# Pack attention with a gated MLP on one core: scores in the banks of h, merged with a chunk of M, and a new written order

## The chip, the cores and the metric

The kernel runs on one core of a Trainium2 chip. The metric is the device time of one launch in microseconds (us). A run of the profiler adds a trace, with the start and duration of every instruction, measured from the first instruction on; that distance from the first to the last instruction is the span. The engines of a core work side by side: TensorE (PE, with the loads of its weights as PEld), VectorE (DVE), ScalarE (ACT), GpSimd (POOL), and SyncE (SP), which here only issues DMAs. Each engine takes its instructions strictly in the order in which the program lists them, and waits on semaphores where it needs something of another.

## The reference

Eight batches, eight heads, 576 positions, head size 64. Packing queries p (32 per head) attend to k and v; the result then serves as keys and values for q. The heads side by side are x, which goes through a gated MLP with 2048 hidden units.

```python
def sm_attn(qq, kk, vv):
    s = scale * np.matmul(qq, kk.transpose(0, 1, 3, 2))
    s = s - np.max(s, axis=-1, keepdims=True)
    a = np.exp(s)
    a = a / (np.sum(a, axis=-1, keepdims=True) + 1e-09)
    return np.matmul(a, vv)
p_packed = sm_attn(p, k, v)
out = sm_attn(q, p_packed, p_packed)
...
h = x @ w_in
g = h * (1.0 / (1.0 + np.exp(-1.702 * h)))
return (g @ w_out).astype(np.float32)
```

## The kernel before

**What it multiplies.** x is never formed. For each batch the packed result P (32 rows per head) is multiplied into w_in first: M = P w_in, four chunks of 512 columns (`m_chunk`, L575). Then h = A M, with A the softmax weights of q (`hp_mm`, L795), and the output is G w_out, with G the gated h (`product`, L868, and `plain`, L874). For accuracy every operand of the large matmuls is split into an upper and a lower rounded part (`..._upper` makes the rounded copy, `..._lower` subtracts it from the value), and each product is three matmuls: hi x hi, hi x lo, lo x hi.

**Rounds.** A batch b has two rounds, n = 2b with 256 positions (even) and n = 2b + 1 with 320 (odd). In a round h is made in eight pairs p of 128 hidden units each (j = 0, 1): two `hp_mm` fill the two banks of the tile `hh`; `hp_tanh` (ACT, L804) reads both, `hp_gate` (DVE, L691) reads both again and leaves G in SBUF; `sums_1`, `sums_2`, `sums_3` (L826, L830, L834) add and subtract blocks of G, since the output is made with seven products in place of eight (a Strassen scheme with the sums of w_out prepared once); `g_upper` (L171 on ACT, L173 on DVE) and `g_lower` (L841) round G and the sums, in two pieces per pair; then come the seven `product` steps, which accumulate in four PSUM banks `acc`. At the end of a round `take_1` to `take_6` (L887 to L911) read `acc`, and `keep` (L917) stores. The odd 64 positions of the odd rounds are laid aside in DRAM (`hp_over`, L814) and go through `product` later in two rounds of their own ("over", read by `over_in`, L818). G and its rounded parts have two buffers each, taken in turn by the pairs; `hh` has one.

**Attention in between.** Of batch b + 1, the packing scores (`scores1`, two halves, L365) are made while the rounds of batch b run: `scores1_copy`, `scores1_max`, `bias1` and `exp1` work on the SBUF tile `x1`, `turn1_blocks` (L480) transposes it in 32-blocks into another tile, and eight DMAs `turn1_out` (L487) with six DMAs `turn1_in` (L498) turn it through DRAM ("aside"). `pack` (L511) multiplies with v, `pack_turn_mm` (L562) transposes P. Then the scores of q (`scores2_mm`, two halves, L617), `scores2_turn` (DVE, L625), `max2`, `sub2`, `exp2`, `sum2`, `norm2`, `turn2`, `a_upper` and `a_lower` make A for the two rounds, and the four `m_chunk` (L583) with `m_upper` (L171, L173) and `m_lower` (L598) make M. From batch 2 on, a chunk of w_in comes by one DMA (`win_in`, L297) into a ring of one buffer.

**Banks.** PSUM has eight banks of 512 columns: 0 to 3 are `acc`, 4 and 5 are h (`hh` once the pairs begin), 6 and 7 are `bb`. From batch 2 on, `scores1`, `scores2_mm`, `m_chunk`, `pack` and `pack_turn_mm` all take turns in 6 and 7.

**PE's tiles.** `hp_mm`, `product` and the like use PE's array as one tile of 128 x 128. `scores1`, `scores2_mm` and `m_chunk` use it as eight tiles of 64 x 32 (four head pairs by even and odd head), `pack` as four of 128 x 32.

**The first batch.** Here nothing runs beside the chain from the loads to the first h matmul: `scores1`, softmax, `turn1_first`, `pack_first`, `scores2_mm`, softmax, `turn2`, `a_upper`, with the first weights decoded by `begin_w` (ACT, L263) and `join_w` (DVE, L276). `warm` (L177) gives PE matmuls on the identity whose results nobody reads. For the first two rounds h is made and multiplied in single pieces (`h_mm`, `out_mm`), while all weights are decoded.

**The order.** The tuple `order` (from L926) lists every step with its engine where there is a choice. The program runs through it once, and each engine's queue is the list filtered for that engine. The order is written out in full, and no scheduler changes it.

```python
for step, *args in order:
    step(*args)
```

Of the kernel before, what the change touches and what calls it, by code (L numbers as in the profile page):

```python
# [24 lines left out]
def kernel(  # L25
# [900 lines left out]
    order = (  # L926
        (load, 'k', 0, 0), (warm, 7, 7, 4), (load, 'k', 0, 1), (load, 'v', 0, 0), (load_w, 0, 0),
        (load, 'v', 0, 1), (load, 'q', 0, 0), (load, 'q', 0, 1), (load_w, 2, 0), (load_w, 1, 0),
        (scores1, 0, 0, (6, 0)), (warm, 1, 1, 5), (load_w, 3, 0), (max1_first, 0, 0),
        (load_w, 2, 1), (max1_first, 1, 0), (load_w, 3, 1), (bias1_first, 0), (bias1_first, 1),  # L930
        (exp1_first, 0, 0), (load_w, 4), (scores1, 0, 1, (7, 1)), (exp1_first, 1, 0),
        (max1_first, 0, 1), (load, 'k', 1, 0), (turn1_first, 0, 6), (bias1, 0, 0), (load_w, 1, 1),
        (max1_first, 1, 1), (exp1_first, 0, 1), (load_w, 0, 1), (bias1, 0, 1), (warm, 3, 3, 4),
        (turn1_first_copy, 0, dve), (factor_first, 0), (factor_first, 1), (load, 'k', 1, 1),
        (exp1_first, 1, 1), (load_w, 7), (turn1_first, 1, 7), (sum1, 0, 1), (load_w, 5),
        (sum1, 0, 0), (load_w, 9), (turn1_last_mm, 0, 6), (turn1_first_copy, 1), (load_w, 6),
        (pack_first, 0), (load_w, 8), (turn1_last_copy, 0), (pack_first, 1), (load_w, 11),
        (pack_first_half, 0), (pack_first, 2), (pack_first_half, 1), (load_w, 10),
        (pack_first_end, 0), (pack_turn_mm, 0, 7), (warm, 6, 2, 5), (pack_turn_copy, 0),
        (begin_w, 0, 0), (scores2_mm, 0, 0, (6, 7)), (warm, 4, 2, 4), (join_w, 0, 0),  # L940
        (scores2_turn, 0, 0, 0), (scores2_mm, 0, 1, (2, 3)), (scores2_turn, 0, 0, 1),
        (warm, 5, 2, 5), (begin_w, 2, 0), (max2, 0, 0, 0), (warm, 8, 3, 4), (max2, 0, 0, 1),
        (begin_w, 1, 0), (scores2_turn, 0, 1, 0), (sub2, 0, 0, 1, pool), (warm, 0, 3, 5),
        (scores2_turn, 0, 1, 1), (sub2, 0, 0, 0, pool), (warm, 2, 3, 4), (max2, 0, 1),
        (exp2, 0, 0, 0), (join_w, 2, 0), (begin_w, 3, 0), (join_w, 1, 0), (exp2, 0, 0, 1),
        (sum2, 0, 0, 0), (begin_w, 3, 1), (join_w, 3, 0), (sum2, 0, 0, 1), (norm2, 0, 0, 0, pool),
        (m_chunk, 0, 0, (0, 1), 0), (m_upper, 0, 0, 1, 0), (sub2, 0, 1, None, pool),
        (turn2, 0, 0, 0), (m_upper, 0, 0, 0, 0), (m_lower, 0, 0, 1, 0), (a_upper, 0, 0, 0),
        (a_lower_mm, 0, 0, 0, 6), (norm2, 0, 0, 1), (exp2, 0, 1), (scores1, 1, 0, (5, 4)),
        (join_w, 3, 1), (turn2, 0, 0, 1), (begin_w, 4), (sum2, 0, 1), (a_upper, 0, 0, 1),  # L950
        (a_lower_copy, 0, 0, 0), (a_lower_mm, 0, 0, 1, 7), (join_w, 4), (scores1_copy, 1, 0, 1),
# [961 lines left out]
```

## Time and profile before

| What | Value |
|---|---|
| Median of three runs | 697.26 us (697.04 to 697.88) |
| Profiled execution, own time | 696.75 us |
| Its span | 694.9 us |
| Mean granted clock of PE | 0.995 |
| PE matmuls of the products, L863 | 349.3 us in 2553 |
| PE matmuls of the pairs, L698 into hh | 203.7 us in 1344 |
| PE matmuls of the chunks of M, L583 into b | 34.4 us in 512 |
| DMA, mean | 148 GB/s |

The page gives each engine's busy time and share of the span, then the 40 slices, the DMA queues, the chain that ended last, and the costliest groups. A group's row reads: line, engine, operation, output<-input with shapes, count | busy time, mean ns of one | idle time just before them and what ended it. A row of the timeline reads: start, duration, engine, line, operation and shapes, count, and in brackets the idle time before it with what ended it. The rows of one group of pipelined matmuls overlap the next by their tails, so the distance from start to start is what a group costs. A row of the waits reads: who waited, for what, the sum in us, how many times, the longest.

### The profile page before, as it was taken

How to read it: one execution, taken by the hardware profiler on the slowest of the kernel's cores; microseconds unless marked ns; L12 is line 12 of the kernel's file. 1: busy time of each engine (PE TensorE's matmuls, PEld its weight loads, DVE VectorE, ACT ScalarE, POOL GpSimd, SP SyncE). 2: the span in 40 equal slices, each digit the busy share in tenths (PEclk: the TensorE clock that was granted, in tenths of full speed). 3: DMA queues.
4: the chain of work that ended last, by engine and by line, in shares of the span. 5: the costliest groups of instructions: out<-in, count | busy, mean ns of one | idle time of the engine just before them, and what ended most of it. 6: DMA issues, size and time to landing. Idle time of an engine off the chain costs nothing. (4 is left out here: it accounts for less than half of the span.)

```text
span 694.9 us, 15468 instructions
## 1 busy us (share of the span) xinstructions
PE 671.4 (97%) x6037; PEld 594.4 (86%) x6037; DVE 594.0 (85%) x1204; ACT 309.5 (45%) x603; POOL 186.6 (27%) x202
## 2 busy tenths in 40 slices
PE   8999999999999999999989999999999999999996
PEld 6678777887879888998789998989889988899996
DVE  5998988968998889978898878998799879988895
ACT  4887645524453444434334434453435434343231
POOL 2543422510761455212331112231112112211010
PEclk9999999999999999999999999999999999999999
DMA  9997961343532545333823334642554353301042
GB/s 344 385 353 223 332 240 61 102 114 116 198 141 60 154 147 210 102 89 137 274 80 92 103 97 133 220 151 45 164 168 162 102 155 103 130 1 43 16 126 60
DMA packets 79016, 103.09 MB, mean 148 GB/s; under 512 B 53920, under 2 KB 58976, under 8 KB 74336
## 3 DMA queue, kind: packets, MB, share of 16 engines
q1 hardware_dynamic: 78944, 102.12, 44.3%
q8 instruction: 47, 0.77, 0.5%
q14 instruction: 25, 0.20, 0.1%
HBM read 80.14 MB, written 21.95 MB: 147 GB/s over the span
## 5 line engine op out<-in xcount | busy, mean ns | idle before, releaser
L863 PE MATMUL acc<-at_float32r 128*128 128x256 f32 (+1 forms) x2553 | 349.3, 292 | 4.7 <-POOL at_float32r L841 1.9
L863 PEld LDWEIGHTS acc<-at_float32r 128*128 128x128 f32 x2553 | 327.5, 192 | 15.2 <-ACT at_float32r L171 2.7
L171 ACT CAST at_float32r<-at_float 128x512 fp32r<-128x512 f32 (+3 forms) x225 | 126.2, 569 | 202.5 <-PE acc L863 101.6
L698 PEld LDWEIGHTS hh<-at_float32r 128*128 128x128 f32 x1344 | 183.8, 189 | 35.0 <-DVE at_float L834 8.2
L698 PE MATMUL hh<-at_float32r 128*128 128x256 f32 (+1 forms) x1344 | 203.7, 300 | 1.6 <-DVE at_float L691 1.5
L841 DVE TENSOR_TENSOR at_float32r<-at_float,at_float32r 128x512 fp32r<-128x512 f32 (+3 forms) x192 | 130.4, 699 | 10.6 <-ACT at_float32r L171 6.6
L804 ACT ACTIVATE at_float<-hh 128x512 f32<-128x512 f32 (+1 forms) x112 | 72.9, 651 | 99.1 <-PE hh L698 93.0
L691 DVE SCALAR_TENSOR_TENSOR at_float<-at_float,hh 128x512 f32<-128x512 f32 (+1 forms) x112 | 83.8, 748 | 27.4 <-ACT at_float L804 27.1
L841 POOL TENSOR_TENSOR at_float32r<-at_float,at_float32r 128x512 fp32r<-128x512 f32 (+3 forms) x49 | 59.0, 1207 | 130.6 <-ACT at_float32r L171 46.9
L826 POOL TENSOR_TENSOR at_float<-at_float 128x256 f32<-128x256 f32 x30 | 22.2, 740 | 157.3 <-DVE at_float L691 154.8
L173 DVE CAST at_float32r<-at_float 128x512 fp32r<-128x512 f32 (+5 forms) x100 | 41.1, 411 | 19.9 <-PE acc L863 15.6
L748 PE MATMUL acc<-at_float32r 128*128 128x512 f32 x192 | 48.1, 393 | 0.0
L598 DVE TENSOR_TENSOR at_float32r<-b,at_float32r 128x512 fp32r<-128x512 f32 (+1 forms) x64 | 41.2, 671 | 1.7 <-ACT at_float32r L171 1.6
L826 DVE TENSOR_TENSOR at_float<-at_float 128x256 f32<-128x256 f32 x83 | 39.0, 470 | 2.4
L748 PEld LDWEIGHTS acc<-at_float32r 128*128 128x128 f32 x192 | 34.8, 188 | 7.0 <-issue 0.8
L830 DVE TENSOR_TENSOR at_float<-at_float 128x128 f32<-128x128 f32 x100 | 34.2, 342 | 4.7 <-POOL at_float L826 1.9
L171 ACT CAST at_float32r<-b 128x512 fp32r<-128x512 f32 (+1 forms) x55 | 29.8, 581 | 17.5 <-PE b L583 17.5
L583 PE MATMUL b<-at_float,at_float 64*32 64x512 f32 (+1 forms) x512 | 34.4, 594 | 0.0
L698 PEld LDWEIGHTS h<-at_float32r 128*128 128x128 f32 x192 | 27.2, 189 | 7.7 <-DVE at_float L625 2.4
L698 PE MATMUL h<-at_float32r 128*128 128x256 f32 (+1 forms) x192 | 30.3, 301 | 1.3 <-DVE at_float L625 0.7
L834 DVE TENSOR_TENSOR at_float<-at_float 128x128 f32<-128x128 f32 x92 | 28.5, 310 | 2.1
L647 POOL TENSOR_TENSOR at_float<-at_float,at_float 128x512 f32<-128x512 f32 (+2 forms) x10 | 10.4, 1045 | 63.3 <-DVE at_float L641 63.3
(117 smaller groups left out, 516.4 us busy)
## 6 DMA issues: line engine op xcount, KB each, us to landing
at_float<-w_kept SPq DMA_DIRECT2D x24, 1024.0 KB, 4.8
at_float<-v SPq DMA_DIRECT2D x8, 1024.0 KB, 4.9
o<-at_float SPq DMA_DIRECT2D x32, 256.0 KB, 2.0
at_float<-w_out SPq DMA_DIRECT2D x16, 511.8 KB, 6.1
at_float<-w_in SPq DMA_DIRECT2D x12, 511.8 KB, 8.3
at_float<-k_last SPq DMA_DIRECT2D x8, 640.0 KB, 6.0
...
```

Of the source, the lines that this page charges most:

```text
L171: nc.scalar.copy(dst, src)
L173: engine.tensor_copy(dst, src)
L583: nc.tensor.matmul(banks[eo][32 * j : 32 * j + 32, columns(part)], pt(b)[rows(eo), j, :], w[rows(eo), j, columns(part)], start=True, stop= ...
L598: nc.vector.tensor_tensor(lo, t[:, at], hi.bitcast(F32), op=ALU.subtract)
L691: nc.vector.scalar_tensor_tensor(dst, th, 1.0, h, op0=ALU.add, op1=ALU.mult)
L698: nc.tensor.matmul(t[:, : NH[half]], m_part(fc, eo, mp)[:, fo : fo + P], a_part(b, half, ap, eo), start=(n == 0), stop=(n == len(terms) - 1),)
L748: nc.tensor.matmul(acc[i], g0(f, gp)[:, i * P : (i + 1) * P], wo(f, wp), start=(start and n == 0), stop=(stop and n == 2),)
L804: nc.scalar.activation(g, h, AF.Tanh, scale=1.702)
L826: engine.tensor_tensor(dst, src, by, op=ALU.subtract)
L830: engine.tensor_tensor(g_raw(n, p, 6), g_raw(n, p, 5), g_raw(n, p, 1), op=ALU.add)
L841: engine.tensor_tensor(lo, src, g_range(n, p, 0, which)[0].bitcast(F32), op=ALU.subtract)
L863: nc.tensor.matmul(acc[i][:, at : at + m], lhs, rhs, start=(start and k == 0), stop=(stop and k == len(pairs) - 1),)
```

## The change

**Banks.** Once `hh` exists, banks 4 and 5 mean its two halves. From batch 2's `scores2_mm` and batch 3's `scores1` on, the scores go there and no longer to 6 and 7. `pack`, `pack_turn_mm` and `m_chunk` stay in 6 and 7.

**Merged steps.** `both` runs two steps directly one after the other. 22 scores (`scores2_mm` of batches 2 to 7, `scores1` of batches 3 to 7, two halves each) are each joined with an `m_chunk` that follows at once: `scores2_mm` of a half with chunks 0 and 1 of the same batch, `scores1` of the next batch with chunks 2 and 3.

**Tiles.** From batch 2 on, the odd heads' first scores `x1` lie in X[3] in place of X[1], and their transposed copy in X[1] in place of X[3].

**Order and engines.** Every other step is the same in kind and number, but the order is another throughout. Products of a pair no longer come in one block of seven; products of two or three pairs mix, and may stand between the two `hp_mm` of a pair. Of the steps with a choice of engine these change: `g_lower` DVE 192 to 159 and POOL 49 to 82; `g_upper` ACT 168 to 144 and DVE 73 to 97; `sums_1` POOL 30 to 41; `sums_2` POOL 13 to 52; `sums_3` POOL 21 to 52; `a_lower` POOL 2 to 8; `sub2` POOL 10 to 13; `m_upper` DVE 10 to 16; `h_over` DVE 1 to 10; some others by a few. At the start, eighteen `warm` matmuls in place of seven stand ahead of the first `scores1`.

The diff, cut: the helpers, the start of the order, the stretch around `pack` and the first scores of batch 5, and the end.

```diff
     def bank(i):
-        return banks_all[i]
+        return pair[0][:, i - 4, :] if pair and i in (4, 5) else banks_all[i]
+
+    def both(*steps):
+        for f, *a in steps:
+            f(*a)
...
     def x1(b, eo):
-        return x_tile(eo)
+        return x_tile((0, 1 if b < 2 else 3)[eo])
+
+    def turned1(b, eo):
+        return x_tile((2, 3 if b < 2 else 1)[eo])
...
     def turn1_blocks(b, eo):
-        nc.vector.transpose(x_tile(2 + eo), x1(b, eo))
+        nc.vector.transpose(turned1(b, eo), x1(b, eo))
...
-        src = x_tile(2 + eo)[NPK * j : NPK * (j + 1), :]
+        src = turned1(b, eo)[NPK * j : NPK * (j + 1), :]
...
     order = (
-        (load, 'k', 0, 0), (warm, 7, 7, 4), (load, 'k', 0, 1), (load, 'v', 0, 0), (load_w, 0, 0),
-        (load, 'v', 0, 1), (load, 'q', 0, 0), (load, 'q', 0, 1), (load_w, 2, 0), (load_w, 1, 0),
-        (scores1, 0, 0, (6, 0)), (warm, 1, 1, 5), (load_w, 3, 0), (max1_first, 0, 0),
...
-        (exp1_first, 0, 0), (load_w, 4), (scores1, 0, 1, (7, 1)), (exp1_first, 1, 0),
...
-        (pack_first_end, 0), (pack_turn_mm, 0, 7), (warm, 6, 2, 5), (pack_turn_copy, 0),
-        (begin_w, 0, 0), (scores2_mm, 0, 0, (6, 7)), (warm, 4, 2, 4), (join_w, 0, 0),
...
-        (warm, 5, 2, 5), (begin_w, 2, 0), (max2, 0, 0, 0), (warm, 8, 3, 4), (max2, 0, 0, 1),
-        (begin_w, 1, 0), (scores2_turn, 0, 1, 0), (sub2, 0, 0, 1, pool), (warm, 0, 3, 5),
-        (scores2_turn, 0, 1, 1), (sub2, 0, 0, 0, pool), (warm, 2, 3, 4), (max2, 0, 1),
...
+        (warm, 1, 1, 5), (load, 'k', 0, 0), (warm, 7, 7, 4), (load, 'k', 0, 1), (load_w, 1, 0),
+        (load_w, 0, 0), (load, 'v', 0, 0), (warm, 6, 2, 5), (load, 'v', 0, 1), (warm, 5, 2, 5),
+        (load, 'q', 0, 0), (warm, 3, 3, 4), (load_w, 2, 0), (warm, 0, 3, 5), (load, 'q', 0, 1),
+        (scores1, 0, 0, (6, 0)), (max1_first, 0, 0), (max1_first, 1, 0), (scores1, 0, 1, (7, 1)),
+        (load_w, 3, 0), (bias1_first, 1), (bias1_first, 0), (exp1_first, 0, 0), (warm, 4, 2, 4),
+        (load_w, 3, 1), (max1_first, 1, 1), (exp1_first, 1, 0), (warm, 8, 3, 4), (bias1, 0, 1),
+        (load_w, 4), (max1_first, 0, 1), (exp1_first, 1, 1), (turn1_first, 0, 6), (bias1, 0, 0),
+        (exp1_first, 0, 1), (begin_w, 1, 0), (turn1_first, 1, 7), (turn1_first_copy, 0, dve),
+        (factor_first, 1), (begin_w, 0, 0), (sum1, 0, 1), (factor_first, 0), (turn1_last_mm, 0, 6),
+        (turn1_first_copy, 1), (load, 'k', 1, 0), (pack_first, 0), (sum1, 0, 0),
...
-        (hp_mm, 9, 2, 1), (take_6, 8), (keep, 8, 1), (turn1_in, 5, 0), (product, 9, 0, 1),
-        (turn1_in, 5, 1), (g_lower, 9, 1, 1, dve), (hp_tanh, 9, 2), (product, 9, 0, 6),
-        (turn1_in, 5, 2), (product, 9, 0, 5), (hp_gate, 9, 2), (turn1_in, 5, 3),
-        (product, 9, 0, 7), (turn1_in, 5, 4), (product, 9, 0, 2), (sums_1, 9, 2, dve),
-        (turn1_in, 5, 5), (product, 9, 0, 3), (product, 9, 0, 4), (sums_2, 9, 2, dve),
-        (hp_over, 9, 2), (sums_3, 9, 2, dve), (hp_mm, 9, 3, 0), (keep, 8, 0),
-        (g_upper, 9, 2, 0, act), (g_upper, 9, 2, 1, dve), (g_lower, 9, 2, 1, dve),
-        (hp_mm, 9, 3, 1), (g_lower, 9, 2, 0, dve), (pack, 5, (6, 7)), (hp_tanh, 9, 3),
...
-        (g_lower, 9, 3, 1, dve), (scores2_mm, 5, 0, (6, 7)), (g_lower, 9, 3, 0, dve),
...
-        (sums_2, 9, 4, dve), (m_chunk, 5, 0, (6, 7), None), (g_upper, 9, 4, 0, act), (sum2, 5, 0),
...
+        (product, 8, 6, 5), (turn1_in, 5, 2), (hp_tanh, 9, 1), (product, 8, 7, 1),
+        (turn1_in, 5, 0), (product, 8, 7, 4), (turn1_in, 5, 4), (hp_gate, 9, 1),
+        (product, 8, 7, 5), (product, 8, 7, 7), (g_lower, 9, 0, 0, dve), (hp_over, 9, 1),
+        (product, 8, 7, 2), (product, 8, 7, 6), (sums_1, 9, 1, pool), (hp_mm, 9, 2, 1),
...
+        (g_lower, 9, 1, 0, pool), (hp_mm, 9, 2, 0), (take_3, 8), (take_6, 8), (sums_2, 9, 1, pool),
+        (hp_tanh, 9, 2), (pack, 5, (6, 7)), (take_4, 8), (sums_3, 9, 1, pool), (keep, 8, 0),
...
+        (product, 9, 3, 2), (g_lower, 9, 2, 1, dve), (product, 9, 1, 6), (product, 9, 1, 3),
+        (sums_1, 9, 4, pool), (both, (scores2_mm, 5, 0, (4, 5)), (m_chunk, 5, 0, (6, 7), None)),
+        (sums_2, 9, 4, pool), (sums_3, 9, 4, pool), (sums_3, 9, 3, pool), (scores2_turn, 5, 0, 0),
+        (m_upper, 5, 0, 1, None, act), (win_in, 5, 1), (product, 9, 2, 6), (scores2_turn, 5, 0, 1),
+        (product, 9, 2, 7), (m_upper, 5, 0, 0, None, act), (g_upper, 9, 4, 0, dve),
+        (product, 9, 1, 5), (hp_mm, 9, 5, 0), (g_lower, 9, 4, 0, dve), (g_upper, 9, 3, 1, act),
...
+        (product, ('over', 1), 7, 6), (product, ('over', 1), 7, 1), (product, ('over', 1), 7, 7),
+        (take_1, ('over', 1)), (product, ('over', 1), 7, 5), (take_2, ('over', 1)),
+        (product, ('over', 1), 7, 3), (take_3, ('over', 1)), (product, ('over', 1), 6, 2),
+        (product, ('over', 1), 7, 2), (take_4, ('over', 1)), (product, ('over', 1), 6, 4),
+        (take_5, ('over', 1)), (product, ('over', 1), 7, 4), (take_6, ('over', 1)),
```

More of the change, by code (lines that the diff above doesn't have):

```diff
@@ L933 @@
[L933 to L938, printed above, removed]
@@ L945 @@
[L945 to L950, printed above, removed]
@@ new lines @@
+        (hp_over, 5, 3), (g_upper, 5, 3, 1, dve), (sums_1, 5, 4, pool), (g_lower, 5, 3, 1, pool),
+        (scores2_turn, 3, 0, 1), (m_upper, 3, 0, 1, None, act), (win_in, 3, 1), (product, 5, 3, 2),
+        (scores2_turn, 3, 0, 0), (product, 5, 2, 1), (m_upper, 3, 0, 0, None, act),
+        (m_lower, 3, 0, 1), (hp_mm, 5, 5, 1), (g_upper, 5, 4, 0, dve), (sums_2, 5, 4, dve),
+        (product, 5, 2, 7), (max2, 3, 0), (hp_mm, 5, 5, 0), (g_lower, 5, 4, 0, dve),
+        (product, 5, 2, 5), (sums_3, 5, 4, dve), (sub2, 3, 0, None, pool), (hp_tanh, 5, 5),
@@ new lines @@
+        (product, 7, 4, 4), (product, 7, 3, 3), (sums_1, 7, 6, dve),
+        (both, (scores2_mm, 4, 1, (4, 5)), (m_chunk, 4, 1, (6, 7), None)), (sums_3, 7, 5, dve),
+        (turn2, 4, 0), (sums_2, 7, 6, pool), (g_lower, 7, 5, 0, dve), (a_upper, 4, 0, None, dve),
+        (m_upper, 4, 1, 1, None, act), (load, 'k', 5, 0), (scores2_turn, 4, 1, 1),
+        (product, 7, 4, 2), (product, 7, 4, 5), (hp_over, 7, 6), (scores2_turn, 4, 1, 0),
+        (g_upper, 7, 5, 1, act), (product, 7, 4, 7), (max2, 4, 1), (win_in, 4, 2),
@@ new lines @@
+        (hp_gate, 11, 4), (product, 11, 2, 5), (product, 11, 2, 2), (g_lower, 11, 3, 0, dve),
+        (both, (scores2_mm, 6, 0, (4, 5)), (m_chunk, 6, 0, (6, 7), None)), (sums_1, 11, 4, dve),
+        (g_upper, 11, 3, 1, dve), (sums_2, 11, 4, pool), (g_lower, 11, 3, 1, pool),
+        (scores2_turn, 6, 0, 1), (win_in, 6, 1), (product, 11, 2, 7), (scores2_turn, 6, 0, 0),
+        (product, 11, 2, 6), (hp_over, 11, 4), (m_upper, 6, 0, 1, None, dve), (product, 11, 2, 4),
+        (hp_mm, 11, 5, 1), (g_upper, 11, 4, 0, act), (max2, 6, 0), (sums_3, 11, 4, dve),
@@ new lines @@
+        (both, (scores2_mm, 7, 1, (4, 5)), (m_chunk, 7, 1, (6, 7), None)),
+        (g_upper, 13, 6, 0, act), (g_lower, 13, 5, 1, dve), (hp_over, 13, 5),
+        (sums_2, 13, 6, pool), (g_lower, 13, 6, 0, pool), (scores2_turn, 7, 1, 1),
+        (m_upper, 7, 1, 0, None, act), (win_in, 7, 2), (product, 13, 4, 6), (product, 13, 5, 2),
+        (scores2_turn, 7, 1, 0), (m_upper, 7, 1, 1, None, act), (hp_mm, 13, 7, 1), (max2, 7, 1),
+        (product, 13, 5, 4), (turn2, 7, 0), (sub2, 7, 1, None, pool), (product, 13, 4, 7),
@@ L1863 @@
+        (take_5, ('over', 1)), (product, ('over', 1), 7, 4), (take_6, ('over', 1)),
+        (keep_over, ('over', 1), 1, 1), (keep_over, ('over', 1), 0, 1),
+        (keep_over, ('over', 1), 0, 0), (keep_over, ('over', 1), 1, 0),
     )
```

1786 lines of the change are left out of this document (882 added, 904 removed).

## The prediction

> **What bounds the kernel now.** I read the page's first block, then PE's waits, then its timeline.
>
> ```profile
> span 694.9 us, 15468 instructions
> PE 671.4 (97%) x6037; PEld 594.4 (86%) x6037; DVE 594.0 (85%) x1204; ACT 309.5 (45%) x603; POOL 186.6 (27%) x202
> ```
> ```profile
> PE b L511 <- DMA at_float<-aside: 5.6, 5, 1.4
> PE acc L863 <- POOL at_float32r L841: 1.9, 3, 0.8
> PE hh L698 <- DVE at_float L691: 1.5, 3, 0.7
> PE acc L863 <- DVE at_float L911: 1.1, 3, 0.4
> ```
>
> TensorE sets the time: 671.4 of 694.9 us. Its largest wait is five times for `turn1_in`'s DMAs before `pack` (5.6 us); the other rows are small. So a change pays only if it shortens PE's own work or removes one of these waits, and costs only where PE is made to wait. What PE's work costs, switches included, shows in the timeline of a steady stretch (start, duration, then the group):
>
> ```profile
> 322.78 2.68 PE L863 MATMUL acc<-at_float32r 128*128 128x256 f32 x21
> 325.30 1.93 PE L698 MATMUL hh<-at_float32r 128*128 128x320 f32 x12
> 327.06 2.68 PE L863 MATMUL acc<-at_float32r 128*128 128x256 f32 x21
> 329.67 1.09 PE L583 MATMUL b<-at_float,at_float 64*32 64x512 f32 x16
> 330.69 2.02 PE L698 MATMUL hh<-at_float32r 128*128 128x320 f32 x12
> 332.55 2.68 PE L863 MATMUL acc<-at_float32r 128*128 128x256 f32 x21
> ```
> ```profile
> 157.87 0.66 PE L617 MATMUL b<-at_float,at_float 64*32 64x256 f32 x16
> 158.47 1.15 PE L698 MATMUL hh<-at_float32r 128*128 128x320 f32 x6
> ```
>
> Seven products (21 matmuls) take 2.52 us from start to start, so one takes 0.36; two `hp_mm` (12) take 1.76. A lone chunk of M (L583) makes the group before it 0.09 longer (2.61 for 2.52), takes 1.02 itself and makes the group after it 0.10 longer (1.86): 1.21. Lone scores of 256 columns (L617) take 0.60, with the same entry and exit 0.79.
>
> **The merged blocks.** All computing steps stay (3512 when `both` is taken apart); only order, engines and places differ. 22 scores now stand directly ahead of a chunk. The kernel before has that pair already, in batch 1, on the same banks:
>
> ```profile
> 73.80 0.66 PE L617 MATMUL h<-at_float,at_float 64*32 64x256 f32 x16
> 74.26 1.06 PE L583 MATMUL b<-at_float,at_float 64*32 64x512 f32 x16
> 75.25 2.03 PE L698 MATMUL h<-at_float32r 128*128 128x320 f32 x12
> 77.12 2.23 PE L748 MATMUL acc<-at_float32r 128*128 128x512 f32 x9
> ```
>
> Scores of 256 columns take 0.46 there, the chunk 0.99, and one entry and exit 0.09 + 0.11: 1.65. Apart they take 0.79 + 1.21 = 2.00. The merge saves 0.35, and 22 x 0.35 = **-7.7 us**. Bounds: 0 (the block waits in front of its banks) to -7.7 (there is no more switching to save). What the merge asks for is that a batch's `scores1` can run while the batch before still uses its second half: its odd part now lies in X[3], no longer in X[1], where `x2` of that half is live until `turn2`. Moving the tile costs no instruction, and `turned1`, now in X[1], is written three pairs of `hp_mm` after `turn2` or later: nothing.
>
> **The aside wait.**
>
> ```profile
> 310.46 1.32 PE L511 MATMUL b<-at_float,at_float 128*32 128x64 f32 x80 [1.20 <-DMA at_float<-aside]
> ```
> ```profile
> at_float<-w_kept SPq DMA_DIRECT2D x24, 1024.0 KB, 4.8
> ```
>
> Between the last `turn1_in` and `pack` stand two `hp_mm` (1.76 us) before, and in batch 5 two products more. After, four to six products stand there: 1.4 to 2.2 us more cover, 0.7 more in batch 5. On SP's queue at most one small `hp_over` lies behind the last `turn1_in`, and as many steps of PE as before lie between the last `turn1_out` and the first `turn1_in`. The longest wait is 1.4 (the row of the waits). The other loads moved on this queue, `win_in` for the next chunk, stand at least 5.5 us of PE's work ahead of it, against 4.8 to land: nothing. Four of five go, the fifth shrinks by 0.7: **-5.1 us** (0 to -5.6).
>
> **The start.**
>
> ```profile
> 1.37 3.36 PE L177 MATMUL h<-at_float 128*128 128x128 f32 x14 [1.37 <-POOL at_float masks.py:199]
> 6.39 0.45 PE L365 MATMUL b<-at_float 64*32 64x320 f32 x1 [0.18 <-DMA at_float<-k_last]
> 14.01 0.49 ACT L263 CAST at_float<-at_float 128x256 f16<-128x256 bf16 x1 [0.78 <-DMA at_float<-w_in]
> 14.85 2.72 PE L177 MATMUL h<-at_float 128*128 128x128 f32 x22
> 22.54 0.38 PE L698 MATMUL h<-at_float32r 128*128 128x256 f32 x1 [0.16 <-ACT at_float L171]
> ```
>
> Until 22.54 the chain of the first batch sets the end, and PE's `warm` matmuls fill. Before, 14 of their matmul records stand ahead of the first scores; after, 36. The 22 more take 2.7 us (row 14.85), so the second scores, held until 6.39 by `k_last`, come at about 7.6: 1.2 later. On ACT two `begin_w` of 0.49 move ahead of the copies that `pack` needs: 1.0. `sub2` of half 0 now goes first on POOL, and joins are done earlier, which gives some back; later `begin_w` cost some. I take **+2.5**; bounds 0 (the chain absorbs it) and +4 (two more 0.49 casts, and 22 records at the first row's 3.36/14 = 0.24 each, 5.3 in place of 2.7). [...]
>
> **The banks of h.** Scores now lie in hh (banks 4, 5), which tanh and gate read. From the first product after a pair's `hp_mm`:
>
> ```profile
> 304.82 2.68 PE L863 MATMUL acc<-at_float32r 128*128 128x256 f32 x21
> 305.07 0.70 ACT L804 ACTIVATE at_float<-hh 128x640 f32<-128x640 f32 x1 [0.16 <-PE hh L698]
> 305.85 0.81 DVE L691 SCALAR_TENSOR_TENSOR at_float<-at_float,hh 128x640 f32<-128x640 f32 x1
> 274.49 2.68 PE L863 MATMUL acc<-at_float32r 128*128 128x256 f32 x21
> 275.50 0.68 DVE L691 SCALAR_TENSOR_TENSOR at_float<-at_float,hh 128x512 f32<-128x512 f32 x1
> ```
>
> hh is free after 306.66 - 304.82 = 1.84 us, with the hand-over of 0.08 (tanh's end to gate) 1.92 in an odd round; 1.7 in an even one. Before, at least seven products (2.52) cover it. After, I count 12 odd pairs with five products or fewer (1.8) to the next `hp_mm`, 9 to the scores (0.12 short), and 3 even ones with four (1.44; 0.26 short): 21 x 0.12 + 3 x 0.26 = 3.3. Behind the scores, `scores2_turn` on DVE must read both banks:
>
> ```profile
> L625 DVE STREAM_TRANSPOSE at_float<-b 128x320 f32<-128x320 f32 x12 | 5.5, 495 | 0.4
> ```
>
> Scores of 320 columns in a merged block are an estimated 0.46 x 320/256 = 0.58. With two transposes of 0.50 and hand-overs of 0.2 that is 1.8, against the scores, the chunk's 0.99 and one product or more: 1.9 at least. It holds. Less the 1.5 us (L691) of now, **+1.8** (-1.5 to +8, if each of the 22 waits 0.3 for DVE's queue).
>
> **Engines and leads.**
>
> ```profile
> L841 DVE TENSOR_TENSOR at_float32r<-at_float,at_float32r 128x512 fp32r<-128x512 f32 (+3 forms) x192 | 130.4, 699 | 10.6 <-ACT at_float32r L171 6.6
> L841 POOL TENSOR_TENSOR at_float32r<-at_float,at_float32r 128x512 fp32r<-128x512 f32 (+3 forms) x49 | 59.0, 1207 | 130.6 <-ACT at_float32r L171 46.9
> L830 DVE TENSOR_TENSOR at_float<-at_float 128x128 f32<-128x128 f32 x100 | 34.2, 342 | 4.7 <-POOL at_float L826 1.9
> L834 POOL TENSOR_TENSOR at_float<-at_float 128x128 f32<-128x128 f32 x21 | 10.4, 496 | 17.4 <-DVE at_float L830 16.6
> ```
>
> 33 `g_lower` and 70 of `sums_2` and `sums_3` go from DVE to POOL: DVE loses 33 x 0.70 + 70 x 0.34 = 47 us, POOL gains 33 x 1.21 + 70 x 0.50 = 75. Neither becomes the bound. But slack goes: from where `g_lower` stands in the order to its first product, PE's steps between come to 4.6 us (median) before, and after to 1.1 to 1.4 where DVE does it, 2.2 where POOL does. PE must wait wherever the operation is late. Nearest row: the wait for POOL L841, 1.9 us in 3. I take **+3** (0 to +23, 226 pieces of G late by 0.1).
>
> **Other waits and the tail.** The takes and the over round: of 1.1 and 1.9, **-2** (0 to -3).
>
> ```profile
> 670.25 18.32 PE L863 MATMUL acc<-at_float32r 128*128 128x256 f32 x150 [0.41 <-DVE at_float L911]
> 686.81 0.37 ACT L887 COPY at_float<-acc 128x256 f32<-128x256 f32 x1 [2.83 <-PE acc L863]
> 689.59 0.41 DVE L911 TENSOR_TENSOR at_float<-acc,at_float 128x256 f32<-128x256 f32 x1
> ```
>
> PE ends at 688.57; the takes start five products earlier and end 1.43 after it. After, seven products lie behind the one that `take_1` needs, two more: **-0.7** (0 to -0.7).
>
> **The sum.** The profiled execution took 696.75 (span 694.9, 1.85 around it): -7.7 - 5.1 + 2.5 + 1.8 + 3 - 2 - 0.7 = -8.2, so 688.6. The median of the runs, 697.26, lies 0.5 above it: **689.1 us**.
>
> **Rivals.** (1) *All of it works*: start, banks and leads cost nothing: 697.26 - 7.7 - 5.1 - 1.5 - 3 - 0.7 = 679.3. For it: all rows of waits but aside's are small now; against: 36 records ahead of the scores. (2) *The merge gives nothing*: each block waits as long on gate as it saves: 689.1 + 7.7 = 696.8, no change. For: hh is one pair; against: rows 73.80 to 77.12. (3) *Slower*: the short leads. POOL holds up DVE:
>
> ```profile
> 277.78 1.58 POOL L684 TENSOR_TENSOR at_float32r<-at_float,at_float32r 128x640 fp32r<-128x640 f32 x1 [0.77 <-ACT at_float32r L171]
> 278.19 2.17 DVE L841 TENSOR_TENSOR at_float32r<-at_float,at_float32r 128x384 fp32r<-128x384 f32 x2
> ```
>
> Two DVE operations, 1.4 us at their line's mean of 0.70, take 2.17 and end 1.0 after POOL's (280.36, 279.36): the first waited for POOL. With 262 us of POOL for 187 this comes more often, and a lead of 1.1 us doesn't hold it. If 226 pieces are late by 0.1 us on average: 689.1 - 3 + 22.6 = 708.7. It turns slower from 0.056 us each on (698.7). Against: DVE has 47 us less to do. [...]
>
> **Chances.** Forecast (684 to 695.8) 0.56, rival 1 0.18, rival 2 0.09, rival 3 0.17. A measurement tells 0.2% (1.4 us). Faster: 0.56 + 0.18 = 0.74; same 0.09; slower 0.17. Range 679 to 702: rival 1 at its lower end, rival 3 up to 0.07 us per piece; the unknown costs' bounds beyond that are left out with about 0.15.
>
> **What would show it.** The L617 to L583 distance at 0.5 with no idle between; no L511 wait on aside, or one; the first h matmul at 25 in place of 22.5; PE's waits for L691 and L841 at 3 us each. Waits for L841, L173 or L171 above 15 us in sum prove rival 3; L617 or L365 waiting for L691 at 0.3 each prove rival 2.

## The result: slower, and the profile after

The changed kernel takes 705.01 us (703.46 to 705.13) against 697.15 us for the kernel before, a ratio of 1.0115 with a 95% interval of 1.0084 to 1.0147: slower by over 1%, where 689.1 was forecast. The profiled execution took 705.11 us. Line numbers moved: L617 became L624, L583 became L590, L698 became L705, L691 became L698, L841 became L848, L863 became L870.

The page of the changed kernel, its first block and the row of the granted clock (each digit a fortieth of the span, in tenths):

```profile
span 703.3 us, 15452 instructions
PE 675.4 (96%) x6037; PEld 602.3 (86%) x6037; DVE 567.5 (81%) x1123; ACT 283.2 (40%) x561; POOL 292.3 (42%) x325
PEclk9699999999999999999999999999999999999999
```

VectorE and GpSimd moved the way that was forecast (594.0 to 567.5, 186.6 to 292.3), though by other amounts: 26.5 us less where 47 had been worked out, and 105.7 more where 75 had. Neither is the bound. New is the 6 in the second slice. TensorE's waits in the changed kernel (total, times, longest):

```profile
PE hh L624 <- DVE at_float L698: 5.0, 6, 1.5
PE hh L705 <- DVE at_float L632: 2.7, 3, 1.9
PE hh L705 <- DVE at_float L698: 2.7, 6, 1.0
PE acc L590 <- DVE at_float L280: 2.3, 1, 2.3
...
PE acc L870 <- DVE at_float32r L848: 0.8, 2, 0.6
```

The wait of `pack` for aside (5.6) is gone whole. In its place stand three rows about the pair of banks hh: scores wait for the gate (5.0), `hp_mm` for the transposes (2.7) and for the gate (2.7, where before had 1.5). Products hardly wait for `g_lower` (0.8).

Two stretches of both kernels, before first and after second, and of the changed kernel also the 3.41 us ahead of its half clock (start:end, length, busy time of PE, PEld, DVE, ACT and POOL, granted clock, share of the DMA engines, GB/s):

```profile
20.00:35.00 15.00, 14.26 (x112) 10.15 (x111) 14.08 (x33) 13.39 (x32) 7.52 (x7) 1.00 0.96 381
35.00:116.00 81.00, 80.34 (x616) 63.91 (x615) 70.97 (x143) 52.26 (x120) 29.17 (x27) 1.00 0.73 258
```
```profile
17.44:20.85 3.41, 1.41 (x18) 0.74 (x16) 3.34 (x11) 1.39 (x4) 1.85 (x4) 1.00 1.04 410
20.00:35.00 15.00, 11.58 (x65) 7.93 (x66) 13.33 (x26) 8.91 (x23) 6.51 (x6) 0.54 0.86 352
35.00:116.00 81.00, 79.41 (x596) 61.31 (x595) 73.68 (x151) 50.12 (x112) 29.34 (x26) 1.00 0.73 242
```

From 20 to 35 us TensorE starts 65 records where it had started 112, at a clock of 0.54: the start lost far more than the delay that was forecast. A **ledger** says how much, and where else. It is worked out from the traces: each matmul is charged what it costs undisturbed (0.120 us for 256 columns and 0.147 for 320, by the rows of 322.78 and 325.30; 0.227 for 512, an estimate on the line of these two, where the traces have a median of 0.230; lone scores 0.79 and 0.89, a lone chunk 1.21, a `pack` 1.46, with 0.19 to 0.20 of entry and exit in each; fillers nothing), and from the start time of each matmul the work charged before it is taken away. What is left is lost time. The work is 654.1 us in all kernels of the table; a merged block lowers the loss, since it is charged as two lone ones.

| lost, us, when this much work is done | 25 | 100 | 300 | 450 | all |
|---|---|---|---|---|---|
| before | 15.4 | 15.8 | 22.3 | 29.7 | 34.1 |
| after | 23.3 | 26.3 | 32.9 | 35.0 | 43.1 |
| after - before, in the stretch | +7.9 | +2.6 | +0.1 | -5.3 | +3.7 |

10.5 us are lost in the first 100 us of work. Behind it the change gains 5.3 around the over round and gives 3.7 back later: -1.5 in all where the forecast had -10.0 (its sum without start and tail). In each of these two stretches one of the profiled executions has 3.41 us of half clock, before from 353.95 and after from 519.20; at the granted clock of 0.50 that withholds an estimated 1.7 us of work each time, so in the sum the two cancel. So two things are to be explained.

### The profile page after: what moved, and what is told of

It reads as the page before. It is cut to its first block, busy times and chain, and to the rows that moved or that the text cites. A ratio compares the mean times of both kernels' runs of the same rounds, so it can differ in the third digit from the quotient of the medians.

```text
span 703.3 us, 15452 instructions
## 1 busy us (share of the span) xinstructions
PE 675.4 (96%) x6037; PEld 602.3 (86%) x6037; DVE 567.5 (81%) x1123; ACT 283.2 (40%) x561; POOL 292.3 (42%) x325
## 4 chain that ended last, share of the span: by engine, by line
PE 46%; DVE 10%; DMA 4%; issue 2%; ACT 2%; POOL 2%; DVEq 0%; SPq 0%; ACTq 0%; POOLq 0%
PE acc L870 28%; PE hh L705 15%; DMA over<-at_float 3%; DVE at_float L698 2%; DVE at_float32r L848 2%; PE b L590 2%; ACT at_float L811 1%; DVE at_float32r L177 1%; DMA at_float<-over 1%; PE hh L624 1%; DVE at_float L900 1%; PE hh L369 1%; DVE at_float32r L605 1%; ACT at_float32r L175 1%; POOL at_float L833 1%
## 5 line engine op out<-in xcount | busy, mean ns | idle before, releaser
L870 PE MATMUL acc<-at_float32r 128*128 128x256 f32 (+1 forms) x2553 | 361.2, 293 | 2.2 <-DVE at_float L918 1.1
L870 PEld LDWEIGHTS acc<-at_float32r 128*128 128x128 f32 x2553 | 330.8, 191 | 31.0 <-issue 14.6
L705 PE MATMUL hh<-at_float32r 128*128 128x256 f32 (+1 forms) x1344 | 208.4, 299 | 5.8 <-DVE at_float L632 2.7
L705 PEld LDWEIGHTS hh<-at_float32r 128*128 128x128 f32 x1344 | 186.9, 190 | 14.4 <-DVE at_float L698 5.4
L811 ACT ACTIVATE at_float<-hh 128x512 f32<-128x512 f32 (+1 forms) x112 | 72.9, 651 | 208.1 <-PE hh L705 132.2
L175 ACT CAST at_float32r<-at_float 128x512 fp32r<-128x512 f32 (+5 forms) x199 | 110.1, 567 | 99.9 <-PE acc L870 47.0
L848 POOL TENSOR_TENSOR at_float32r<-at_float,at_float32r 128x512 fp32r<-128x512 f32 (+3 forms) x82 | 102.3, 1251 | 91.3 <-DVE at_float32r L177 45.8
L698 DVE SCALAR_TENSOR_TENSOR at_float<-at_float,hh 128x512 f32<-128x512 f32 (+1 forms) x112 | 84.0, 750 | 56.9 <-ACT at_float L811 54.6
L848 DVE TENSOR_TENSOR at_float32r<-at_float,at_float32r 128x512 fp32r<-128x512 f32 (+3 forms) x159 | 109.4, 699 | 10.5 <-ACT at_float32r L175 7.1
L177 DVE CAST at_float32r<-at_float 128x512 fp32r<-128x512 f32 (+5 forms) x126 | 56.0, 449 | 8.6 <-PE acc L870 2.9
L837 POOL TENSOR_TENSOR at_float<-at_float 128x128 f32<-128x128 f32 x52 | 27.9, 537 | 82.5 <-DVE at_float L833 72.3
L833 POOL TENSOR_TENSOR at_float<-at_float 128x256 f32<-128x256 f32 x41 | 34.1, 831 | 62.6 <-DVE at_float L698 43.0
L841 POOL TENSOR_TENSOR at_float<-at_float 128x128 f32<-128x128 f32 x52 | 27.5, 529 | 46.4 <-DVE at_float L837 44.3
L605 DVE TENSOR_TENSOR at_float32r<-b,at_float32r 128x512 fp32r<-128x512 f32 (+1 forms) x64 | 41.9, 669 | 1.4 <-ACT at_float32r L175 1.3
L833 DVE TENSOR_TENSOR at_float<-at_float 128x256 f32<-128x256 f32 x72 | 33.7, 468 | 4.6 <-DMA at_float<-over 1.5
L705 PEld LDWEIGHTS h<-at_float32r 128*128 128x128 f32 x192 | 30.0, 203 | 7.5 <-DVE at_float L698 2.3
L705 PE MATMUL h<-at_float32r 128*128 128x256 f32 (+1 forms) x192 | 32.8, 315 | 2.5 <-DVE at_float32r L605 1.1
L590 PE MATMUL b<-at_float,at_float 64*32 64x512 f32 (+1 forms) x512 | 34.6, 586 | 0.0
L280 DVE SCALAR_TENSOR_TENSOR at_float<-at_float,at_float 128x512 uint32<-128x512 uint32 (+1 forms) x36 | 29.7, 848 | 2.1 <-ACT at_float L267 2.0
```

The source lines that it names most:

```text
L175: nc.scalar.copy(dst, src)
L177: engine.tensor_copy(dst, src)
L280: nc.vector.scalar_tensor_tensor(dec(n)[:, at].bitcast(U32), raw(n)[:, at, 0], 13, tops[(n + (part or 0)) % 4][:, at], op0=ALU.logical_shi ...
L590: nc.tensor.matmul(banks[eo][32 * j : 32 * j + 32, columns(part)], pt(b)[rows(eo), j, :], w[rows(eo), j, columns(part)], start=True, stop= ...
L605: nc.vector.tensor_tensor(lo, t[:, at], hi.bitcast(F32), op=ALU.subtract)
L698: nc.vector.scalar_tensor_tensor(dst, th, 1.0, h, op0=ALU.add, op1=ALU.mult)
```

## Experiments

Theory A: the start lost it, through the fillers ahead of the scores, casts in front of the chain, and the clock. Theory C, formed from the traces of the first runs: behind the start, G's buffers come free late, so tanh and gate are late, and the merged scores that share hh wait. Against them stand the prediction's rivals 2 (the merge gives nothing) and 3 (short leads and GpSimd's hold on VectorE). Each run is compared with runs of the kernel before on its own chip (medians 696.6 to 697.6).

| run | us | ratio to before, 95% |
|---|---|---|
| s1_warm_back | 703.19 | 1.0088 (1.0066 to 1.0110) |
| s2_before_front | 699.84 | 1.0036 (1.0018 to 1.0053) |
| s3_before_start | 698.50 | 1.0025 (1.0011 to 1.0039) |
| s4_more_warm | 705.23 | 1.0116 (1.0095 to 1.0136) |
| s5_over_first | 694.87 | 0.9974 (0.9959 to 0.9988) |
| s6_turn_first | 700.09 | 1.0041 (1.0027 to 1.0055) |
| s7_split | 705.14 | 1.0113 (1.0094 to 1.0132) |
| s8_engines | 728.62 | 1.0441 (1.0420 to 1.0463) |
| s9_casts | 702.74 | 1.0092 (1.0071 to 1.0112) |
| s10_turn_one | 692.35 | 0.9936 (0.9920 to 0.9952) |
| s11_long | 689.90 | 0.9897 (0.9879 to 0.9915) |
| s12_clock | 702.10 | 1.0073 (1.0049 to 1.0097) |
| s13_after_steady | 698.23 | 1.0010 (0.9996 to 1.0025) |
| s14_prefix58 | 699.04 | 1.0025 (1.0008 to 1.0042) |
| s14_prefix107 | 695.60 | 0.9983 (0.9967 to 0.9999) |

### The fillers, from both sides

The edit of s1_warm_back; s2_before_front is the reverse in the kernel before:

```diff
-(warm, 1, 1, 5),
 (warm, 7, 7, 4),
-(warm, 6, 2, 5), (warm, 5, 2, 5), (warm, 3, 3, 4), (warm, 0, 3, 5),
 (scores1, 0, 0, (6, 0)),
+(warm, 1, 1, 5),
...
 (turn1_first, 0, 6),
+(warm, 3, 3, 4),
...
 (scores2_mm, 0, 1, (2, 3)),
+(warm, 5, 2, 5), (warm, 8, 3, 4), (warm, 0, 3, 5), (warm, 2, 3, 4),
```

> The changed kernel with its 25 warm matmuls at the places that they had in the kernel before: 7 ahead of the first scores, the others behind them; every other step as in the changed kernel. Theory A (the start lost the time: fillers ahead of the scores hold the chain up, and their lack later halves PE's clock): first scores at about 4.7 us in place of 8.35, first h matmul at 23 to 24 in place of 26.78, no stretch of half clock between 20 and 34 us, about 695 (705.0 - 10). Rival B (the steady part lost it: short leads, or waits of the merged blocks): at most the 3.7 us of the fillers come back, 701 or more, and the waits behind 100 us stay.

> The kernel before with its 25 warm matmuls at the places of the changed kernel: 18 ahead of the first scores. Theory A: 36 records in front, first scores at 8.3, first h matmul at 25.5 to 27, half clock in a stretch around 20 to 34 us, 704 to 707 (697.2 + 7 to 10). Rival B: only the delay of the chain, no half clock, 699 to 701.

Put back, they gain 1.8 us of 705.0, hardly more than the noise; put in front of the kernel before, they cost it 0.36%, 2.5 us. The prediction had 1.2 for them, by second scores at 7.6; in the changed kernel these start at 8.80, 2.4 later than the 6.39 of before. Both runs have the first scores near where theory A put them (4.66 and 7.64). Both also have a stretch of half clock, 6.83 us from 23.8 and from 19.4, which theory A had for the second alone. But neither moves the time by the 7 to 10 us of theory A: the fillers are a quarter of it.

### The start as a whole, and more fillers

The edit of s3_before_start (s11_long and s14 are of the same kind, with other lengths):

```diff
 order = (
-(warm, 1, 1, 5), (load, 'k', 0, 0), (warm, 7, 7, 4), (load, 'k', 0, 1), (load_w, 1, 0),
+(load, 'k', 0, 0), (warm, 7, 7, 4), (load, 'k', 0, 1), (load, 'v', 0, 0), (load_w, 0, 0),
...
```

> The changed kernel with the first 147 steps of the kernel before, in their order and on their engines (all that stands up to the second half of the first chunk of M); all other steps in the order of the changed kernel. Theory A: the start of before with the rest of after: first h matmul at 22.5, no half clock there, 694 to 695.5 (705.0 - 10.5). Rival B: 701 or more, since the time is lost behind it.

The edit of s4_more_warm:

```diff
-(warm, 2, 3, 4)
+(warm, 2, 15, 4)
```

> The changed kernel with 12 warm matmuls more (24 records, about 2.9 us at full clock) between the second scores2 and the first chunk of M, where PE was idle for 2.31 us; all else as changed. It parts the two halves of theory A: the chain stays as late (first h matmul at 26 to 27), but the idle time is filled. If the half clock of 20.6 to 34.3 us comes from that idle time and costs about 5 us, it goes, and the time is 699 to 701; if the half clock has another cause or costs nothing, 704 to 706.

The start of before gains 6.5 us, with the first h matmul at 22.33 and no half clock in the start: most of the loss is there, though 698.5 is 3 above what was expected, since this order loses 2 us more at the seam and gains nothing later (ledger: 18.2 at 100 us of work, 36.5 at the end). More fillers gain nothing: the half clock is shorter (6.83 for 13.65 us) and comes later, and the time stays, 705.2.

### Behind the start: why the gate is late

In the changed kernel tanh (L811) reads hh and writes the raw words of G, of which there are two sets, for pairs p and p-2 in turn. What ended ScalarE's idle time ahead of tanh, from 150 us on, other than `hp_mm`; the changed kernel first, then the one before:

```profile
  DVE at_float32r L848: 23.1, 8
  DMA over<-at_float: 14.7, 4
  DVE at_float L841: 6.3, 2
...
  POOL at_float L841: 5.1, 2
```
```profile
its engine sat idle before it (us, times) until:
...
  ACT at_float32r L171: 2.9, 5
  issue: 1.3, 1
```

Before, none of these waits is put down to another engine or a DMA (the five for L171 are for ScalarE's own casts). After, some 17 are: tanh waits for `g_lower` and sums of pair p-2, and for `hp_over`'s DMA, which reads that pair's remainder. The longest one, with the queue of SP, ScalarE and TensorE:

```profile
571.41 0.56 SPq L821 DMA_DIRECT2D over<-at_float  x1
572.01 0.61 SPq L227 DMA_DIRECT2D at_float<-q  x1
572.72 0.85 SPq L924 DMA_DIRECT2D o<-at_float  x2
573.62 4.62 SPq L821 DMA_DIRECT2D over<-at_float  x2
```
```profile
581.47 0.70 ACT L811 ACTIVATE at_float<-hh 128x640 f32<-128x640 f32 x1 [4.68 <-DMA over<-at_float]
```
```profile
583.08 0.67 PE L624 MATMUL hh<-at_float,at_float 64*32 64x256 f32 x16 [1.51 <-DVE at_float L698]
```

The DMA to over is issued at 573.6 behind 512 KB of q and two writes of o, tanh of the pair after next starts at 581.47, and the merged scores stand still for 1.51 us until gate has read hh. The next run moves only such DMAs up.

```diff
 (hp_gate, 13, 2),
+(hp_over, 13, 2),
...
 (load, 'q', 7, 0),
...
 (keep, 12, 0), (keep, 12, 1),
-(hp_over, 13, 2),
...
```

> From here on the base is the changed kernel with the first 147 steps of before (698.5 us, 1.0025 of before). Here 12 of its hp_over steps move up on SP's queue, ahead of the loads of q and the writes of o (keep) that stood between them and their gate; nothing else moves. Theory C (tanh of pair p writes the buffer of G that pair p-2 had, and waits until that pair's DMA to over has landed; gate and with it the merged scores come late): the waits of tanh for over's DMA (14.1 us in 5) go, TensorE's waits of scores2 for gate fall from 3.9 to under 2, and the time is 696.0 to 697.0 (698.5 - 2). Rival (gate is late through its own queue on VectorE): 698 to 699, and the waits for gate stay.

694.87: 3.6 us gained, more than expected, from twelve DMAs of 64 KB that change place on a queue. Its trace shows no wait of tanh for over's DMA and this row of TensorE's waits, where its base had 3.9:

```profile
PE hh L624 <- DVE at_float L698: 2.0, 4, 0.8
```

That row explains 1.9 of the 3.6 us; the rest shows in no row of waits, though the base's profiled execution had 3.41 us of half clock at 510.91 that this one has not. The waits of tanh for `g_lower` on VectorE stay (23.2 us in 8). No run takes these alone away, so what they cost is not shown.

The other late reader of hh is the pair of transposes behind the scores. At 514 us of the changed kernel, VectorE, GpSimd and TensorE:

```profile
514.90 1.23 DVE L837 TENSOR_TENSOR at_float<-at_float 128x128 f32<-128x128 f32 x1 [0.63 <-POOL at_float L833]
516.05 0.41 DVE L177 CAST at_float32r<-at_float 128x512 fp32r<-128x512 f32 x1
516.39 0.70 DVE L671 STREAM_TRANSPOSE at_float<-at_float 128x512 f32<-128x512 f32 x1
517.02 0.87 DVE L632 STREAM_TRANSPOSE at_float<-hh 128x320 f32<-128x320 f32 x2
```
```profile
514.84 1.15 POOL L848 TENSOR_TENSOR at_float32r<-at_float,at_float32r 128x448 fp32r<-128x448 f32 x1
```
```profile
517.94 2.27 PE L705 MATMUL hh<-at_float32r 128*128 128x320 f32 x11 [1.93 <-DVE at_float L632]
```

VectorE waits for a sum that the change gave to GpSimd, then its own sum takes 1.23 us beside GpSimd's `g_lower`, where such a sum took 0.34 before, and only then come the transposes. `hp_mm` waits 1.93.

The edit of s10_turn_one, which s6_turn_first makes at all twelve places:

```diff
 (both, (scores2_mm, 6, 1, (4, 5)), (m_chunk, 6, 1, (6, 7), None)),
+(scores2_turn, 6, 1, 1), (scores2_turn, 6, 1, 0),
 (g_upper, 11, 6, 0, act), (sums_2, 11, 6, dve),
...
 (turn2, 6, 0),
-(scores2_turn, 6, 1, 1),
...
-(scores2_turn, 6, 1, 0),
```

> The base with both scores2_turn of each of the 12 batches' halves directly behind their merged block on VectorE's queue, ahead of the sums, g_lower and turn2 that stood before them. Theory: the wait of hp_mm for the transposes (2.7 us in 3, the longest 1.9 at 510 us, and the 3.41 us of half clock behind it) goes, since VectorE stood still for POOL's sums_1 and then ran sums_2 slowed by POOL ahead of the transposes: 698.5 - 2.4 - 1.7 = 694.5, or 695.5 if something else comes late by a third of it. Rival (the work pushed back is late for the products in its place): 698 to 700, with new waits of products for L848 or L177.

> The run with hp_over moved up (694.9 us), and the two scores2_turn of batch 6's second half alone directly behind their merged block. Theory: of the 12 places, only here VectorE was so late (1.9 us), so moving this one pair gains what moving all twelve lost elsewhere: 694.9 - 1.9 = 693.0, 692.5 to 693.8. Rival (what is pushed back comes late in turn, as in the run with all twelve): 694.5 to 695.5.

With all twelve pairs moved the wait for L632 goes, but the time is 700.09, 1.6 more, hardly clear of the noise and no gain: the rival held. The waits for gate grow by 0.8 in the scores and 1.8 in `hp_mm`, those for L848 by 1.5. With the one pair moved that was late by 1.9, the time is 692.35, 2.5 better. The remedy is right only where it was needed.

### The merge, and the engines

One of the 22 places of s7_split, and a few steps of s8_engines:

```diff
-(both, (scores1, 3, 0, (4, 5)), (m_chunk, 2, 2, (6, 7), None)),
+(scores1, 3, 0, (4, 5)), (product, 3, 6, 7), (m_chunk, 2, 2, (6, 7), None),
...
```

> The base with one product between the scores and the chunk of M in each of the 22 blocks (in 13 the product behind the block, in 9 the one ahead of it, where the scores come 0.36 us earlier), same banks. It undoes the merge alone. If the merge saves 0.33 us a time: 698.5 + 22 x 0.33 = 705.8, 704.5 to 706.5. If the merge gives nothing (rival 2): 698 to 699.

```diff
-(sums_1, 4, 4, pool),
+(sums_1, 4, 4, dve),
...
-(g_upper, 4, 4, 0, dve),
+(g_upper, 4, 4, 0, act),
...
```

> The base, each step at its place in the order, but on the engine that it had in the kernel before (473 steps change engine, among them 63 g_lower and 113 sums from POOL to VectorE, 30 g_lower and 32 sums back). [...] Theory C (the order costs it: G of a pair is read so late that the pair after next waits): within 2 us of 698.5, or more where before's engines don't fit this order, and tanh's waits for L848 and L841 stay above 30 us in sum.

One product between scores and chunk costs 6.6 us, 0.30 for each of 22 blocks (1.2 us of it are longer waits about hh): the merge gives nearly what was forecast. Rival 2, by which each block waits as long as it saves, is out; but six of the 22 blocks do wait for gate, 5.0 us together. A block in the changed kernel, with its neighbours:

```profile
191.82 1.24 PE L870 MATMUL acc<-at_float32r 128*128 128x256 f32 x9
193.04 0.67 PE L369 MATMUL hh<-at_float 64*32 64x256 f32 x16
193.49 1.07 PE L590 MATMUL b<-at_float,at_float 64*32 64x512 f32 x16
194.49 0.62 PE L870 MATMUL acc<-at_float32r 128*128 128x256 f32 x3
```

From scores to chunk are 0.45 us, and the chunk takes 1.00, as in the pair of before at 73.80. Had the new engines cost the time, the old ones would have come out below the 698.50 of s3_before_start, the base here. Before's engines in this order take 728.62, 30 us more, with VectorE at 592.6 us and TensorE's wait of `hp_mm` for gate at 8.0. One part of the expectation missed: tanh's waits for L848 and L841 do not stay above 30 us but fall to 6.4, and the kernel is slower all the same. Rival 3 is out as well: in this order the new engines do not cost the time, the order needs them. What they would cost in an order made for the old engines no run shows.

### The rest of the start

```diff
-(join_w, 3, 1),
...
 (m_upper, 0, 0, 1, 0, act),
+(m_upper, 0, 0, 0, 0, act),
...
-(begin_w, 0, 1), (begin_w, 4), (join_w, 0, 1), (join_w, 4), (m_upper, 0, 0, 0, 0, act), (begin_w, 1, 1),
...
 (m_lower, 0, 0, 0, 0),
+(join_w, 3, 1), (begin_w, 0, 1), (join_w, 0, 1), (begin_w, 4), (join_w, 4), (begin_w, 1, 1),
```

> The run with the fillers back (703.2 us), and beside it six weight casts and joins (begin_w and join_w of the second halves and of chunk 1) behind m_upper and m_lower of the first chunk on ScalarE and VectorE, where they stood ahead of them. Theory A (the rest of the start's loss is the first h matmuls waiting behind casts that nobody needs yet): the waits of the first h matmuls for ScalarE (1.4) and for m_lower (1.0) go, first h matmul at 22.7 to 23.5 in place of 24.26, the half clock of 23.6 to 30.4 us goes or is halved, 698.5 to 700.5. Rival (the order of the loads makes it late): 702 to 704, first h matmul still at 24.

The same with fillers:

```diff
 (m_chunk, 0, 0, (0, 1), 0),
+(warm, 9, 3, 2),
...
 (scores1, 1, 0, (5, 4)),
+(warm, 9, 1, 2),
...
 (h_mm, 0, 0, 0, 4),
+(warm, 9, 3, 2),
...
 (scores1, 1, 1, (6, 7)),
+(warm, 9, 5, 2),
```

> The run with the casts moved (702.7 us), and 15 warm matmuls more (30 records) in TensorE's gaps between the first chunk of M and the second group of h, in a bank that is free there; nothing else moves. It keeps the chain and takes the half clock alone away. If the half clock of 25.6 to 32.4 us follows from the thin window ahead of it (TensorE busy 0.48 of 22.2 to 25.6) and costs what it withholds: no half clock before the tail, 702.7 - 3.4 = 699.3, 698.3 to 700.3. If it costs nothing, since other engines set the end there: 702 to 703.5.

With the casts moved, the first h matmul comes at 21.80, ahead of the kernel before, and its waits go; yet the time falls by 0.5 only, which is within the noise and where the rival had the time, though not the first h matmul. The casts now hold up what follows (four `begin_w` in 2.06 us from 23.75 on ScalarE, and h matmuls that wait 1.1 for a copy behind them), and the half clock comes at 25.9. With fillers in those gaps the profiled execution has no half clock in the start any more, and the time is 702.1: 0.6 less, or 1.3 by the ratios to before, and neither is clear of the noise. The traces tell more: the fillers make the first h matmul 0.8 later (22.63), and yet the group of h that starts at 92.92 without them starts at 92.60 with them. So the half clock of 6.83 us cost an estimated 1.1 us of the 3.4 that it withheld. Theory A's second half, 5 us for 13.65 us of it, is borne out neither here nor in s4_more_warm. The half clock of s9_casts cost little: TensorE waits there for VectorE and ScalarE anyway (3.3 us in four rows of waits).

What was left is divided by the length of the piece taken from the kernel before, with hp_over and the one pair of transposes put right throughout:

> The changed kernel with its own start, hp_over moved up as before and the one pair of scores2_turn of batch 6 moved up: only what was found behind the start. If the two causes are independent, it gains what they gained on the base: 705.0 - 3.6 - 2.5 = 698.9, 698 to 700; the start still costs its 8 to 10. If the start's loss is what made them late, it gains under 2: 703 or more.

> The changed kernel with what was found behind its start (698.2 us), and the first 58 steps of before: all up to the transpose of the first pack, with the loads of before; the fillers behind it at before's places. With 147 steps of before the same kernel takes 692.4. If the loss lies in the fillers and the loads ahead of pack: 693 to 694.5. If it lies in the order of casts, joins and copies behind pack: 696 to 697.5 (the fillers' 1.8 alone).

> The same with the first 107 steps of before: also the second scores, the softmax of the first batch, the first chunk of M and its weight casts, up to the copies of the lower part of A. If the order from pack to the first h is the rest: 692 to 693, as with 147 steps. If the order of the first h round (scores1_copy, begin_w, h_upper, a_lower) is: 695.5 to 697.

> As the run before, but with the first 590 steps of the kernel before in place of 147 (all of its start and of its first rounds, up to about 116 us), since the ledger shows that the changed order loses 2 us more in that stretch: 18.2 lost at 100 us of work where before had lost 15.8. Theory: 693.0 - 2.4 = 690.6, 690 to 692. Rival (the loss at the seam comes back behind it): 693.

| steps of before in front | 0 | 58 | 107 | 147 | 590 |
|---|---|---|---|---|---|
| us | 698.23 | 699.04 | 695.60 | 692.35 | 689.90 |

Run s13 shows that the two causes are independent: on the changed kernel with its own start the two edits gain 6.8 us (6.1 on the base) and bring it level with before. The first 58 steps, with their loads and fillers, then gain nothing, which neither expectation had; from `pack` to the first h 3.4 us, in the first h round 3.3, behind it 2.4. One thing that 147 steps put right and 107 do not shows in three rows of each, VectorE, GpSimd and TensorE; s14_prefix107 first, then s10_turn_one:

```profile
23.09 2.06 DVE L280 SCALAR_TENSOR_TENSOR at_float<-at_float,at_float 128x256 uint32<-128x256 uint32 x2 [0.23 <-ACT at_float L267]
```
```profile
23.00 1.26 POOL L668 TENSOR_TENSOR at_float<-at_float,at_float 128x640 f32<-128x640 f32 x1 [2.34 <-DVE at_float L664]
```
```profile
25.86 1.44 PE L705 MATMUL h<-at_float32r 128*128 128x256 f32 x5 [1.80 <-DVE at_float32r L605]
```
```profile
22.53 0.63 DVE L280 SCALAR_TENSOR_TENSOR at_float<-at_float,at_float 128x512 uint32<-128x512 uint32 x1
23.07 0.41 DVE L605 TENSOR_TENSOR at_float32r<-acc,at_float32r 128x256 fp32r<-128x256 f32 x1
```
```profile
22.76 1.52 POOL L668 TENSOR_TENSOR at_float<-at_float,at_float 128x640 f32<-128x640 f32 x1 [2.34 <-ACT at_float L175]
```
```profile
23.54 1.64 PE L705 MATMUL h<-at_float32r 128*128 128x256 f32 x11 [0.42 <-DVE at_float32r L605]
```

Two joins of weights that nobody needs yet stand ahead of `m_lower` (L605) on VectorE, just when GpSimd runs `norm2`. They take 2.06 us, and h waits 1.80 for `m_lower`. In the other kernel one join starts before `norm2`, takes 0.63, and h waits 0.42. That is 1.4 of the 3.3 us. The changed kernel has two such joins too, and one wait more; its rows of TensorE and VectorE, and those of before:

```profile
21.16 0.64 PE L590 MATMUL acc<-at_float,at_float 64*32 64x256 f32 x2 [2.31 <-DVE at_float L280]
25.66 2.04 DVE L280 SCALAR_TENSOR_TENSOR at_float<-at_float,at_float 128x256 uint32<-128x256 uint32 x2
```
```profile
18.57 0.62 PE L583 MATMUL acc<-at_float,at_float 64*32 64x256 f32 x4 [0.42 <-DVE at_float L276]
16.70 0.75 DVE L276 SCALAR_TENSOR_TENSOR at_float<-at_float,at_float 128x256 uint32<-128x256 uint32 x2
```

The first chunk of M waits 2.31 us for a join that comes later than before; with the fillers put back (s1_warm_back) that wait is gone.

s11_long beats both kernels: 689.90 us, 1.03% below before. Its ledger reads 15.8, 16.2, 22.3, 23.8 and 26.3.

## Why the prediction was wrong, step by step

- **Merge, -7.7.** Right: 6.6 by undoing it, 0.30 a block for 0.35.
- **Aside wait, -5.1.** Right: all five waits are gone, 5.6.
- **Start, +2.5.** Wrong, and the larger failure: +10.5 in the ledger, 8.3 in the time (698.23 to 689.90). The term for the fillers was too small: 1.2, where the two runs that moved them show 1.8 and 2.5. The larger part failed at "joins are done earlier, which gives some back": two early joins stand ahead of `m_lower` on VectorE, and beside GpSimd's softmax they take 2.04 us (2.06 in s14_prefix107), where two took 0.75 in the kernel before. The first h matmul came at 26.78, where 25 was forecast and put down as the test. The runs place 3.4 us from `pack` to the first h, 3.3 in the first h round and 2.4 behind it. Which steps cost them stays open beyond that one place (1.4 us): moving six casts and joins alone gained 0.5, within the noise.
- **The halved clock.** The sum has no term for it. It came, for 13.65 us, behind 3.41 us in which TensorE was busy for 1.41 (17.44 to 20.85). The run that took 6.83 us of it away gained 0.6, not clear of the noise.
- **Banks of h, +1.8.** Wrong, the second failure. The three rows about hh sum to 10.4 us, 8.9 more than the 1.5 of before. The step took hh to be free 1.92 us after the first product behind `hp_mm`; that supposes that tanh starts at once. Tanh's own destination, G's words of pair p-2, was not in the working. Moving the DMAs to over that hold it gained 3.6 us, moving the late pair of transposes 2.5.
- **Engines and leads, +3.** Right that G is drained later, wrong about who waits. Products hardly do (L848: 0.8); tanh waits, then gate, then the scores. Going back to the old engines in this order costs 30 us.
- **Other waits, -2, and tail, -0.7.** The over round gave 5.3 with its merged blocks, up to 1.7 of it the half clock of the kernel before. From TensorE's end to the last operation 0.73 us for 1.43: -0.7.
- **The sum.** Without start and tail -10.0 was forecast; the ledger has -1.5. By the runs and the rows of waits the merge gave -6.6, aside -5.6, the banks +8.9, and products waiting for `g_lower`, `g_upper` and the takes -2.7 (4.6 us before, 1.9 after): -6.0. So the banks were 7.1 worse than forecast and the other terms together 3.1 better, and 4.5 us lie in gaps too short for a row of waits. Part of these shows in the traces: behind the first 100 us of work, waits and half clock left out, a matmul of 256 columns takes 0.1227 us to the start of the next on full tiles where it took 0.1218 before, some 2.4 us in sum. Why stays unnamed. Rival 3 had the sign and nearly the size (708.7), but not the mechanism: its rows (L841, L173, L171 above 15 us) never came. What it feared, VectorE held up by GpSimd, is seen at 514.9 (1.23 us for 0.34) and at the joins (2.04 for 0.75).

That s11_long lands at 689.9 against the forecast's 689.1 is no merit of the forecast: it has the start of before and two edits that the change did not have.
